# Reading the moving operand of one-pass products from two halves in turn

## The chip, the cores and the metric

The kernel runs on one core of one Trainium2 chip. The metric is the device time of one execution in microseconds (us). Engines are named as the profile names them: PE is the matrix engine (TensorE), PEld its weight loads, DVE the vector engine, ACT the scalar engine, POOL the GpSimd engine, SP the engine that issues most transfers. L977 is line 977 of the kernel before.

## The reference

Two stages follow each other. First a long convolution with a filter that a small network makes, gated by x:

```python
h_filt = (np.maximum(pos_emb @ w1, 0.0) @ w2) * np.exp(-0.01 * pos)[:, None]
u = x * v                                   # x, v: [2, 12480, 128]
y = irfft(rfft(u, 2 * S) * rfft(h_filt, 2 * S))[:, :S]
z = x * y                                   # [24960, 128] after a reshape
```

Then an MLP with a leaky ReLU on every row of z:

```python
h = z @ w_in                                # [24960, 128] @ [128, 2048]
g = np.maximum(0.01 * h, h)
out = g @ w_out                             # [24960, 2048] @ [2048, 128]
```

Everything is float32.

## The kernel before

The convolution is done as a transform over 98 x 128 points in two steps, a product with the filter's spectrum, and the way back. Batch 0's convolution and the filter's spectrum fill the time up to about 337 us. From there on the MLP runs, and the rest of the convolution (batch 1 and the last inverse transforms) is woven between the MLP's steps.

The MLP works on 50 column tiles of tokens: 46 of 512 columns and four ends of 390, 314, 352 and 352 (`widths`). For each tile it makes 16 steps, one for every 128 of the 2,048 hidden units. A step has two parts. `m1` multiplies the tile by 128 columns of `w_in`, and the result is passed through the ReLU on ACT and split into a high part `rh` and a low part `rl`. `m2`, issued three steps later (`DEEP`), multiplies `rh` and `rl` by `w_out` and adds into the tile's accumulator `acc`. Every operand is held as a high and a low float32r part, so each logical product is three products on PE: high by high, high by low, low by high. [...] The other products (`conv1`, `fwd`, `back_halves`, `last_transform`, the transposes) use plain float32 operands; the rows below show what one of their columns takes.

For 21 of the 50 tiles (`sums(k)`) the leaky ReLU is split as 0.99 relu(h) + 0.01 h, with the second term folded into three products by `wc_h` and `wc_l` (L1006 to L1008). There ACT writes `rh` straight from PSUM (L981) and DVE makes `rl` from PSUM and `rh` (L982). For the other 29 tiles ACT makes `r` from PSUM (L990), and ACT or DVE casts it to `rh` (L994, L992); DVE makes `rl` from the two (L995) without reading PSUM.

The result of a tile stands in `acc`. `finish` copies it on ACT in pieces (L1025) into tiles `ot` of 390 tokens, which PE transposes back to rows (L1037) and SP stores.

Batch 1's second convolution stage (`conv1b`) has two places with one-pass products, both through `three` (L138): the forward product `up`, read by ACT and DVE at L522, L524 and L528, and the way back, `back`, whose result ACT copies at L210 in `back_evac`.

The order is written out by hand: a program order for each engine, with `pace` handing out the pieces of batch 1's convolution among the MLP's steps, and tables (`ends`, `turn_at`, `gets`) that place the last transforms.

Of the kernel before, what the change touches and what calls it, by code (L numbers as in the profile page):

```python
# [12 lines left out]
AF = mybir.ActivationFunctionType  # L13
# [17 lines left out]
def tile_conv_mlp(ctx, tc, x, v, pos_emb, w1, w2, w_in, w_out, cf, cr, cg, cb, ci, cw, out):  # L31
# [81 lines left out]
            pass  # L113


    def chunk(c):
        k0 = c * KC
        return k0, min(KC, NA - k0)
# [27 lines left out]
    def back_halves(dp, pin, c):  # L146

        for j, w in halves(c):
            for s in range(2):
                rows = slice(HB * s, HB * s + HB)  # L150
                for ri in range(2):
                    nc.tensor.matmul(dp[s][:, w], mi2[j][rows, ri, :], pin[rows, ri, w],
                                     start=(ri == 0), stop=(ri == 1))

    def back(dp, parts, c):

        for s in range(2):
            for j, w in halves(c):
                three(dp[s][:, w], (mi_h[j][:, s], mi_l[j][:, s]), (parts[0][:, s, w], parts[1][:, s, w]))

    def turned(pool, psum, m2, m1):

# [39 lines left out]
    def store_back(b, c, ct, eng):  # L202
        k0, n = chunk(c)
        eng.dma_start(out=scr2[b][k0:k0 + n].rearrange("k r m e -> (r m) k e"),
                          in_=ct[:, :n].rearrange("p k s d -> p k (s d)"))

    def back_evac(dp, ct, n):

# [5 lines left out]
    with tc.manual_schedule():  # L214
# [237 lines left out]
        def conv1b():  # L452

            pool = psc["pool"]
            hd, parts = {}, {}

            def fetch_b(c):
                if c < NCH:
                    k0, n = chunk(c)
                    got[c] = s0.tile([128, 1024], F32, tag="s1", name="bin1", bufs=3).rearrange(  # L460
                        "p (k s d) -> p k s d", s=2, d=D)
                    nc.sync.dma_start(out=got[c][:, :n].rearrange("p k s d -> p k (s d)"),
                                      in_=scr1b[:, k0:k0 + n, :])

            def fetch_h(c):
                n = chunk(c)[1]
                h = pool.tile([128, 2, 2, 512], F32, tag="hd", name="hd")
                for i in range(2):
                    nc.sync.dma_start(out=h[HB * i:HB * i + HB, :, :, :n * D], in_=hspec[c][:, :, :, :n * D])
                hd[c] = h  # L470

            def split(c):
                _, n = chunk(c)
                t = got.pop(c)
                th = pool.tile([128, KC, 2, D], F32R, tag="th", name="th", bufs=1)
                tl = pool.tile([128, KC, 2, D], F32R, tag="tl", name="tl", bufs=1)
                parts[c] = th, tl
                nc.scalar.copy(th[:, :n, 0, :], t[:, :n, 0, :])
                yield
                for s in range(2):  # L480
                    if s == 0:
                        nc.scalar.copy(th[:, :n, 1, :], t[:, :n, 1, :])
                    nc.vector.tensor_tensor(out=tl[:, :n, s, :], in0=t[:, :n, s, :], in1=th[:, :n, s, :],
                                            op=ALU.subtract)
                    yield

            def sums(us, p1, h, s, w):
                nc.gpsimd.tensor_tensor(out=us[:, s, :w], in0=us[:, s, :w], in1=h[:, 1, s, :w], op=ALU.mult)
                nc.gpsimd.tensor_tensor(out=p1[:, s, :w], in0=p1[:, s, :w], in1=us[:, s, :w], op=ALU.add)

            fetch_b(0)
            fetch_h(0)
            fetch_b(1)
            fetch_b(2)
            for _ in range(WAIT):
                yield
            yield from split(0)
            late, pins = None, {}
            for c in range(NCH + 1):
                if c + 1 < NCH:  # L500
                    fetch_h(c + 1)
                if late:
                    late()
                    late = None
                if c < NCH:
                    n = chunk(c)[1]
                    w = n * D
                    h, (th, tl) = hd.pop(c), parts.pop(c)
                    yield
                    up = psc["next"]()  # L510
                    for s in range(2):
                        three(up[s][:, :w].rearrange("p (k d) -> p k d", d=D), (mb_h[:, s], mb_l[:, s]),
                              (th[:, :n, s, :], tl[:, :n, s, :]))
                    yield

                    us, p1 = sc.tile([128, 2048], F32, tag="s4", name="usp").rearrange(
                        "a (i s w) -> i a s w", i=2, s=2)
                    ph = pool.tile([128, 2, 512], F32R, tag="ph", name="ph", bufs=1)
                    pl = pool.tile([128, 2, 512], F32R, tag="pl", name="pl", bufs=1)
                    pins[c] = ph, pl  # L520
                    for s in range(2):
                        nc.scalar.mul(us[L, s, :w], up[s][H, :w], -1.0)  # L522
                        o = 1 - s
                        nc.vector.tensor_tensor(out=p1[:, o, :w], in0=up[o][:, :w], in1=h[:, 0, o, :w], op=ALU.mult)  # L524
                        if s:
                            sums(us, p1, h, 0, w)
                        yield
                        nc.scalar.copy(us[H, s, :w], up[s][L, :w])  # L528
                        yield
                    sums(us, p1, h, 1, w)  # L530
                if c + 1 < NCH:
                    yield from split(c + 1)
                    fetch_b(c + 3)
                if c:
                    wb = chunk(c - 1)[1] * D
                    dp = psc["next"]()
                    back(dp, pins.pop(c - 1), c - 1)
                    yield
                    ct = pool.tile([128, KC, 2, D], F32, tag="ct1", name="ct1", bufs=1)
                    yield from back_evac(dp, ct, wb // D)  # L540
                    late = lambda c=c, ct=ct: store_back(1, c - 1, ct, nc.sync)
                    yield
                if c < NCH:
                    for s in range(2):
                        nc.scalar.copy(ph[:, s, :w], p1[:, s, :w])
                        nc.gpsimd.tensor_tensor(out=pl[:, s, :w], in0=p1[:, s, :w], in1=ph[:, s, :w],
                                                op=ALU.subtract)
                        yield
            late()
# [419 lines left out]

        def m1(k, f):  # L970
            w = widths[k]
            zh, zl = (i[:, :w] for i in z[k])
            hp = ps.tile([128, WIDE], F32, tag="mh", name="mh", bufs=3)[:, :w]
            fs = slice(f * 128, f * 128 + 128)
            for i, (u, m) in enumerate(((w_in_h, zh), (w_in_l, zh), (w_in_h, zl)) if k == f == 0 else
# [2 lines left out]
            rh = sm.tile([128, WIDE], F32R, tag="rh", name="rh", bufs=DEEP + 2)[:, :w]  # L978
            rl = sm.tile([128, WIDE], F32R, tag="rl", name="rl", bufs=DEEP + 2)[:, :w]
            if sums(k):  # L980
                nc.scalar.activation(out=rh, in_=hp, func=AF.Relu)  # L981
                nc.vector.scalar_tensor_tensor(out=rl, in0=hp, scalar=0.0, in1=rh, op0=ALU.max, op1=ALU.subtract)  # L982
            else:
                tag, pool, bufs = ((("th", psc["pool"], 1), ("tl", psc["pool"], 1), ("ct1", psc["pool"], 1),
                                    ("ph", psc["pool"], 1), ("pl", psc["pool"], 1)) if k in OWN else
                                   (("s1", s0, 3), ("hd", psc["pool"], 2), ("ct1", psc["pool"], 1),
                                    ("s1", s0, 3), ("hd", psc["pool"], 2)))[f % 5]
                r = pool.tile([128, 2048 if tag == "hd" else 1024], F32R if tag in ("th", "tl", "ph", "pl") else F32,
                              tag=tag, name="r", bufs=bufs)[:, :w].bitcast(F32)
                nc.scalar.activation(out=r, in_=hp, func=AF.Lrelu, alpha=0.01)  # L990
                if f % 2:
                    nc.vector.tensor_copy(rh, r)  # L992
                else:
                    nc.scalar.copy(rh, r)  # L994
                nc.vector.tensor_tensor(out=rl, in0=r, in1=rh, op=ALU.subtract)  # L995
            return rh, rl

        def m2(k, f, r):
            rh, rl = r
            w = widths[k]  # L1000
            if f == 0:
                acc[k] = ps.tile([128, WIDE], F32, tag=f"acc{k % 2}", name="acc", bufs=1)
            if f == 0 and sums(k):
                zh, zl = (i[:, :w] for i in z[k])
                ap = acc[k][:, :w]
                nc.tensor.matmul(ap, wc_h, zh, start=True, stop=False)  # L1006
                nc.tensor.matmul(ap, wc_h, zl, start=False, stop=False)
                nc.tensor.matmul(ap, wc_l, zh, start=False, stop=False)  # L1008
# [7 lines left out]
        def finish(k):  # L1016
# [3 lines left out]
            for t in range(at0[k] // TOK, (at0[k + 1] - 1) // TOK + 1):  # L1020
                for kk, a, c, n in pieces_of(t):
                    if kk == k:
                        if t not in ots:
                            ots[t] = sm.tile([128, TOK], F32, tag="ot", name="ot", bufs=3)
                        nc.scalar.copy(ots[t][:, c:c + n], ap[:, a:a + n])  # L1025
                        if c + n == TOK:
                            whole.append(t)
            for t in whole:
# [243 lines left out]
```

## Time and profile before

| | |
|---|---|
| median of three executions | 1689.55 us (1683.47 to 1690.23) |
| the profiled execution's own time | 1684.68 us |
| its span, first to last instruction | 1682.9 us |
| mean granted TensorE clock | 0.988 |
| busy: PE, PEld, DVE, ACT, POOL | 97%, 78%, 71%, 60%, 49% |

The span is what the trace covers; 1.8 us of the execution lie outside of it. A row of the trace gives an instruction's line, engine, operation, output and inputs by the program's names, and its shape: `128*128 128x512` is a product with 128 x 128 weights and 512 moving columns. The end of a matrix product is modelled, and one product starts before the one ahead of it has ended, so a product's own duration (0.39 us) is not what it costs: the distance from one start to the next is.

### The profile page before, as it was taken

How to read it: one execution, taken by the hardware profiler on the slowest of the kernel's cores; microseconds unless marked ns; L12 is line 12 of the kernel's file. 1: busy time of each engine (PE TensorE's matmuls, PEld its weight loads, DVE VectorE, ACT ScalarE, POOL GpSimd, SP SyncE). 2: the span in 40 equal slices, each digit the busy share in tenths (PEclk: the TensorE clock that was granted, in tenths of full speed). 3: DMA queues.
4: the chain of work that ended last, by engine and by line, in shares of the span. 5: the costliest groups of instructions: out<-in, count | busy, mean ns of one | idle time of the engine just before them, and what ended most of it. 6: DMA issues, size and time to landing. Idle time of an engine off the chain costs nothing.

```text
span 1682.9 us, 27337 instructions
## 1 busy us (share of the span) xinstructions
PE 1628.1 (97%) x9173; PEld 1319.2 (78%) x9173; DVE 1193.9 (71%) x1785; ACT 1008.0 (60%) x2056; POOL 821.6 (49%) x804
## 2 busy tenths in 40 slices
PE   6897999899999999999999999999999999999999
PEld 6786555488888888888888888888888888887888
DVE  4775888656775566666566664887887887878765
ACT  1332454345654577676677676666667676676666
POOL 3563212245643376767567763654464545445410
PEclk9998999999999999999999999999999999999999
DMA  8898999766766466656566631321212212121100
GB/s 237 285 301 248 342 321 342 253 195 186 209 177 196 124 170 196 192 157 171 155 177 165 167 105 55 122 68 56 61 61 66 75 53 75 56 61 56 56 11 20
DMA packets 166357, 253.30 MB, mean 151 GB/s; under 512 B 14302, under 2 KB 119026, under 8 KB 163146
## 3 DMA queue, kind: packets, MB, share of 16 engines
q1 hardware_dynamic: 146478, 226.29, 45.6%
q10 hardware_dynamic: 19740, 25.28, 4.3%
q8 instruction: 73, 1.20, 0.3%
q14 instruction: 66, 0.54, 0.1%
HBM read 168.00 MB, written 83.43 MB: 149 GB/s over the span
## 4 chain that ended last, share of the span: by engine, by line
PE 79%; DVE 9%; DMA 7%; issue 2%; ACT 1%; SPq 1%; POOL 0%; ACTq 0%; DVEq 0%; POOLq 0%
PE mh L977 30%; PE acc L1011 10%; PE acc L1012 10%; PE acc L1010 10%; PE cv L138 4%; PE yp L903 4%; PE cv L425 3%; DMA scr<-o 2%; DMA ft<-in_cf_dram 2%; PE op L1037 2%; PE zp L922 1%; PE up L124 1%; DVE rl L995 1%; DVE ta L132 1%; PE a L381 1%
## 5 line engine op out<-in xcount | busy, mean ns | idle before, releaser
L995 DVE TENSOR_TENSOR rl<-r,rh 128x512 fp32r<-128x512 f32 (+2 forms) x464 | 398.1, 875 | 101.0 <-ACT rh L994 92.4
L990 ACT ACTIVATE r<-mh 128x512 f32<-128x512 f32 (+2 forms) x464 | 271.3, 586 | 193.8 <-PE mh L977 175.2
L982 DVE SCALAR_TENSOR_TENSOR rl<-mh,rh 128x512 fp32r<-128x512 f32 (+1 forms) x336 | 227.8, 683 | 222.9 <-ACT rh L981 220.6
L977 PE MATMUL mh<-zh,w_in_h 128*128 128x512 f32 (+3 forms) x800 | 327.6, 410 | 0.8 <-ACT zh L966 0.7
L1011 PE MATMUL acc<-rl,w_out_h 128*128 128x512 f32 (+3 forms) x800 | 309.6, 387 | 1.3 <-DVE rl L995 0.6
L977 PE MATMUL mh<-zh,w_in_l 128*128 128x512 f32 (+3 forms) x800 | 310.3, 388 | 0.0
L1010 PE MATMUL acc<-rh,w_out_h 128*128 128x512 f32 (+3 forms) x800 | 310.3, 388 | 0.0
L1012 PE MATMUL acc<-rh,w_out_l 128*128 128x512 f32 (+3 forms) x800 | 309.9, 387 | 0.0
L977 PE MATMUL mh<-zl,w_in_h 128*128 128x512 f32 (+3 forms) x800 | 309.4, 387 | 0.0
L981 ACT ACTIVATE rh<-mh 128x512 fp32r<-128x512 f32 (+1 forms) x336 | 199.7, 596 | 157.3 <-PE mh L977 151.4
L936 POOL TENSOR_TENSOR zl<-zf,zh 128x390 fp32r<-128x390 f32 (+24 forms) x110 | 69.3, 643 | 406.1 <-ACT zh L935 401.0
L666 POOL TENSOR_TENSOR cp<-cq,cp 98x256 f32<-98x256 f32 x248 | 223.0, 899 | 34.4 <-DVE cp L654 17.7
L992 DVE CAST rh<-r 128x512 fp32r<-128x512 f32 (+2 forms) x232 | 146.5, 632 | 48.6 <-ACT r L990 47.3
L1011 PEld LDWEIGHTS acc<-rl,w_out_h 128*128 128x128 f32 x800 | 150.3, 188 | 38.5 <-DVE rl L995 7.0
L977 PEld LDWEIGHTS mh<-zh,w_in_l 128*128 128x128 f32 x800 | 150.7, 188 | 32.1
L977 PEld LDWEIGHTS mh<-zh,w_in_h 128*128 128x128 f32 x800 | 151.2, 189 | 31.1 <-issue 3.9
L1012 PEld LDWEIGHTS acc<-rh,w_out_l 128*128 128x128 f32 x800 | 150.3, 188 | 30.7
L1010 PEld LDWEIGHTS acc<-rh,w_out_h 128*128 128x128 f32 x800 | 150.4, 188 | 30.2
L977 PEld LDWEIGHTS mh<-zl,w_in_h 128*128 128x128 f32 x800 | 151.5, 189 | 24.1 <-DVE zl L968 0.2
L994 ACT CAST rh<-r 128x512 fp32r<-128x512 f32 (+2 forms) x232 | 140.9, 607 | 7.3
L663 POOL TENSOR_TENSOR cq<-cin 98x256 f32<-98x256 f32 x124 | 120.1, 968 | 0.8 <-DMA cin<-scr 0.8
L654 POOL TENSOR_TENSOR cp<-cin 98x256 f32<-98x256 f32 x78 | 74.6, 975 | 66.3 <-PE yp L903 32.0
(165 smaller groups left out, 2390.1 us busy)
## 6 DMA issues: line engine op xcount, KB each, us to landing
cin<-scr SPq DMA_DIRECT2D x318, 98.0 KB
hd<-hspec SPq DMA_DIRECT2D x48, 512.0 KB
bin<-scr SPq DMA_DIRECT2D x23, 768.0 KB
scr<-o SPq DMA_DIRECT2D x28, 588.0 KB
scr<-ct SPq DMA_DIRECT2D x25, 512.0 KB
scr1b<-o SPq DMA_DIRECT2D x32, 392.0 KB
hspec<-hs ACTq DMA_DIRECT2D x48, 256.0 KB
xm<-in_x_dram SPq DMA_DIRECT2D x128, 96.0 KB
```

The costliest lines, as they stand in the source:

```text
L663: eng.tensor_tensor(out=cq[:, p], in0=ci_t[:, 0, :, 0, :], in1=ci_t[:, 0, :, 1, :], op=op)
L666: eng.tensor_tensor(out=cp[:, p, w], in0=cq[:, p], in1=cp[:, p, 1], op=op)
L977: nc.tensor.matmul(hp, u[:, fs], m, start=(i == 0), stop=(i == 2))
L981: nc.scalar.activation(out=rh, in_=hp, func=AF.Relu)
L982: nc.vector.scalar_tensor_tensor(out=rl, in0=hp, scalar=0.0, in1=rh, op0=ALU.max, op1=ALU.subtract)
L990: nc.scalar.activation(out=r, in_=hp, func=AF.Lrelu, alpha=0.01)
L992: nc.vector.tensor_copy(rh, r)
L994: nc.scalar.copy(rh, r)
L995: nc.vector.tensor_tensor(out=rl, in0=r, in1=rh, op=ALU.subtract)
L1010: nc.tensor.matmul(ap, w_out_h[:, f, :], rh, start=(f == 0 and not sums(k)), stop=False)
L1011: nc.tensor.matmul(ap, w_out_h[:, f, :], rl, start=False, stop=False)
L1012: nc.tensor.matmul(ap, w_out_l[:, f, :], rh, start=False, stop=(f == NF - 1))
```

## The change

Three helpers are added. `mixed` reads a tile of 2n columns in the order 0, n, 1, n+1, ...; `plain` takes a result that stands in that order in PSUM and gives it back as two halves, each read with a step of two; `split2` is the same pair of halves on a tile in plain order.

```diff
+    def mixed(t):
+        return t.rearrange("p (h i) -> p i h", h=2)
+    def plain(t):
+        return t.rearrange("p (i h) -> p h i", h=2)
+    def split2(t):
+        return t.rearrange("p (h i) -> p h i", h=2)
+    def even(w):
+        return (w.stop - w.start) // D % 2 == 0
```

In the MLP the moving operands of all products are read through `mixed`, and all that read their results do it through `plain`:

```diff
         def m1(k, f):
-            zh, zl = (i[:, :w] for i in z[k])
+            zh, zl = (mixed(i[:, :w]) for i in z[k])
...
-                nc.scalar.activation(out=rh, in_=hp, func=AF.Relu)
-                nc.vector.scalar_tensor_tensor(out=rl, in0=hp, scalar=0.0, in1=rh, op0=ALU.max, op1=ALU.subtract)
+                nc.scalar.activation(out=split2(rh), in_=plain(hp), func=AF.Relu)
+                nc.vector.scalar_tensor_tensor(out=split2(rl), in0=plain(hp), scalar=0.0, in1=split2(rh),
+                                               op0=ALU.max, op1=ALU.subtract)
...
-                nc.scalar.activation(out=r, in_=hp, func=AF.Lrelu, alpha=0.01)
+                nc.scalar.activation(out=split2(r), in_=plain(hp), func=AF.Lrelu, alpha=0.01)
...
         def m2(k, f, r):
-            rh, rl = r
+            rh, rl = (mixed(i) for i in r)
...
-                zh, zl = (i[:, :w] for i in z[k])
+                zh, zl = (mixed(i[:, :w]) for i in z[k])
...
-                        nc.scalar.copy(ots[t][:, c:c + n], ap[:, a:a + n])
+                        half = widths[k] // 2
+                        for h in range(2):
+                            lo, hi = max(a, half * h), min(a + n, half * h + half)
+                            if lo < hi:
+                                nc.scalar.copy(ots[t][:, c + lo - a:c + hi - a],
+                                               plain(ap[:, :2 * half])[:, h, lo - half * h:hi - half * h])
```

In `conv1b` the same is done for the forward products and, where a group holds an even number of 128-column blocks, for the products of the way back:

```diff
-                        three(up[s][:, :w].rearrange("p (k d) -> p k d", d=D), (mb_h[:, s], mb_l[:, s]),
-                              (th[:, :n, s, :], tl[:, :n, s, :]))
+                        three(up[s][:, :w], (mb_h[:, s], mb_l[:, s]),
+                              [i[:, :n, s, :].rearrange("p (h k) d -> p k d h", h=2) for i in (th, tl)])
...
-                        nc.scalar.mul(us[L, s, :w], up[s][H, :w], -1.0)
+                        nc.scalar.mul(split2(us[L, s, :w]), plain(up[s][H, :w]), -1.0)
-                        nc.vector.tensor_tensor(out=p1[:, o, :w], in0=up[o][:, :w], in1=h[:, 0, o, :w], op=ALU.mult)
+                        nc.vector.tensor_tensor(out=split2(p1[:, o, :w]), in0=plain(up[o][:, :w]),
+                                                in1=split2(h[:, 0, o, :w]), op=ALU.mult)
-                        nc.scalar.copy(us[H, s, :w], up[s][L, :w])
+                        nc.scalar.copy(split2(us[H, s, :w]), plain(up[s][L, :w]))
...
     def back(dp, parts, c):
-                three(dp[s][:, w], (mi_h[j][:, s], mi_l[j][:, s]), (parts[0][:, s, w], parts[1][:, s, w]))
+                m = mixed if even(w) else lambda t: t
+                three(dp[s][:, w], (mi_h[j][:, s], mi_l[j][:, s]), (m(parts[0][:, s, w]), m(parts[1][:, s, w])))
```

`mixed_evac` takes the place of `back_evac` there: the same copies, with a step of two where the group is even; the one chunk that is cut into odd groups gets two copies for each half instead of one.

## Rows read from the trace of the kernel before

**Rows 1.** The page, part 1: busy time and share of the span.
```profile
PE 1628.1 (97%) x9173; PEld 1319.2 (78%) x9173; DVE 1193.9 (71%) x1785; ACT 1008.0 (60%) x2056; POOL 821.6 (49%) x804
```

**Rows 2.** Windows: stretch, length, busy time and instructions, granted clock, DMA share, GB/s.
```profile
core 0: us, PE busy (x) PEld busy (x) DVE busy (x) ACT busy (x) POOL busy (x), PEclk, DMA share, GB/s
184.00:188.00 4.00, 3.73 (x40) 2.34 (x37) 2.51 (x5) 2.41 (x6) 1.29 (x1) 1.00 0.99 366
600.00:700.00 100.00, 100.00 (x502) 81.54 (x501) 63.32 (x92) 70.59 (x145) 71.41 (x71) 1.00 0.69 190
1200.00:1300.00 100.00, 99.90 (x504) 81.33 (x503) 80.19 (x103) 70.02 (x141) 47.05 (x51) 1.00 0.19 56
```

**Rows 3.** Groups by line and form, whole span: count, busy us, mean ns, idle before.
```profile
L977 PE MATMUL mh<-zh,w_in_h 128*128 128x512 f32 x736 | 304.9, 414 | 0.1
L1006 PE MATMUL acc<-zh,wc_h 128*128 128x512 f32 x20 | 7.8, 392 | 0.0
L977 PE MATMUL mh<-zh,w_in_h 128*128 128x352 f32 x32 | 10.6, 330 | 0.0
L138 PE MATMUL cv<-th,mb_h 128*128 128x512 f32 x48 | 19.3, 402 | 0.0
L138 PE MATMUL cv<-ph,mi_h 128*128 128x512 f32 x46 | 18.6, 403 | 0.0
```

**Rows 4.** Timeline, PE, two MLP steps (start us, duration us): first and last product.
```profile
1199.80 0.39 PE L977 MATMUL mh<-zh,w_in_h 128*128 128x512 f32 x1
...
1202.32 0.39 PE L1012 MATMUL acc<-rh,w_out_l 128*128 128x512 f32 x1
```

**Rows 5.** Timeline, PE: from the first `up` product to what follows the sixth.
```profile
588.20 0.40 PE L138 MATMUL cv<-th,mb_h 128*128 128x512 f32 x1
...
589.59 0.39 PE L977 MATMUL mh<-zh,w_in_h 128*128 128x512 f32 x1
```

**Rows 6.** Timeline, PE, 352 columns: the first and the ninth of a run.
```profile
1664.02 0.32 PE L1010 MATMUL acc<-rh,w_out_h 128*128 128x352 f32 x1
...
1665.30 0.32 PE L1012 MATMUL acc<-rh,w_out_l 128*128 128x352 f32 x1
```

**Rows 7.** Timeline, PE: float32 products merged, and what starts after them.
```profile
184.98 1.94 PE L124 MATMUL up<-bin,mb 128*64 128x512 f32 x8 [0.27 <-DVE ta L132]
186.72 1.07 PE L769 MATMUL ep<-mb,bin 128*64 128x128 f32 x16
...
383.37 1.91 PE L425 MATMUL cv<-xv,ft 98*98 98x128 f32 x16
385.04 0.47 PE L977 MATMUL mh<-zh,w_in_h 128*128 128x512 f32 x1
```

**Rows 8.** Groups by form: readers of PSUM (first four), then DVE in the weights' preparation.
```profile
L990 ACT ACTIVATE r<-mh 128x512 f32<-128x512 f32 x325 | 195.3, 601 | 147.1 <-PE mh L977 132.9 <-DVE rl L995 2.3
L990 ACT ACTIVATE r<-mh 128x352 f32<-128x352 f32 x32 | 15.0, 468 | 7.7 <-PE mh L977 7.7
L982 DVE SCALAR_TENSOR_TENSOR rl<-mh,rh 128x512 fp32r<-128x512 f32 x161 | 109.9, 689 | 100.3 <-ACT rh L981 99.7
L982 DVE SCALAR_TENSOR_TENSOR rl<-mh,rh 128x390 fp32r<-128x390 f32 x16 | 8.9, 563 | 7.4 <-ACT rh L981 7.2
L91 DVE SCALAR_TENSOR_TENSOR fs<-wo,fa 128x256 uint32<-128x256 uint32 x8 | 3.4, 426 | 0.3
L98 DVE TENSOR_TENSOR wo<-fa,fb 128x256 f32<-128x256 f32 x8 | 3.4, 425 | 0.3
```

**Rows 9.** Groups by form: ACT in 600 to 900 us, then DVE in 1100 to 1600 us.
```profile
L522 ACT ACTIVATE usp<-cv 64x512 f32<-64x512 f32 x34 | 20.3, 597 | 2.6 <-PE cv L138 1.6
...
L995 DVE TENSOR_TENSOR rl<-r,rh 128x512 fp32r<-128x512 f32 x324 | 290.0, 917 | 58.0 <-ACT rh L994 51.8
L992 DVE CAST rh<-r 128x512 fp32r<-128x512 f32 x163 | 109.3, 671 | 36.6 <-ACT r L990 35.9
```

**Rows 10.** Waits in total (us, times, longest), and the last copy in the timeline.
```profile
PEld acc L1011 <- DVE rl L995: 7.0, 15, 0.7
...
1678.25 0.45 ACT L1025 COPY ot<-acc 128x352 f32<-128x352 f32 x1 [1.61 <-PE acc L1012]
```

More of the change, by code (lines that the diff above doesn't have):

```diff
@@ L205, in store_back, with mixed_evac @@
                           in_=ct[:, :n].rearrange("p k s d -> p k (s d)"))
+    def mixed_evac(dp, ct, c):
+        for s in range(2):
+            for _, w in halves(c):
+                o, i = ct[:, w.start // D:w.stop // D, s, :], dp[s][:, w]
+                if even(w):
+                    nc.scalar.copy(o.rearrange("p (h k) d -> p h k d", h=2),
+                                   i.rearrange("p (k d h) -> p h k d", h=2, d=D))
+                else:
+                    nc.scalar.copy(o, i.rearrange("p (k d) -> p k d", d=D))
+            yield
     def back_evac(dp, ct, n):
@@ L539, in conv1b @@
                     ct = pool.tile([128, KC, 2, D], F32, tag="ct1", name="ct1", bufs=1)
-                    yield from back_evac(dp, ct, wb // D)
+                    yield from mixed_evac(dp, ct, c - 1)
                     late = lambda c=c, ct=ct: store_back(1, c - 1, ct, nc.sync)
```

## The prediction

> **What bounds the kernel now.** I read the busy times first, then the windows, then the starts of PE's products in the timeline, and last the groups of those that read PE's results. PE is busy for 97% of the span, the next engine, DVE, for 71% [rows 1]. [...]
>
> What a product costs is the distance between starts. Twelve of the MLP's products of 512 columns start within 1199.80 to 1202.32 us, eleven distances: 2.52 / 11 = 0.2291 us each [rows 4]. [...]
>
> [...]
>
> **The change part by part.**
>
> *The order in which products read.* Each product reads as many columns as before, now n, n+256, n+1, ... [...] The count: six lines of 736 products of 512 columns and three of 20 [rows 3] make 4,476, each 13.1 ns shorter: 58.6 us. The conv products, three of 48 and three of 46 [rows 3], 282 in all, from 231.7 to 216: 4.4 us. The 192 of 352 columns (six of 32 [rows 3]) from 160 to 148.5, the same price for a column: 2.2 us. The tiles of 390 and 314, 96 products and a few each, at some 10 ns (an estimate by their width): 2 us. Together 67 us. [...]
>
> [...]
>
> *The readers of PSUM with a step of two.* ACT reads each MLP result once (L981 or L990), DVE those of 21 tiles too (L982), and ACT and DVE the convolution's. ACT pays (601 - 468) / 160 = 0.83 ns a column and DVE (689 - 563) / 122 = 1.03 [rows 8]. Below, the step costs nothing: DVE reads 256 words with a step of two at L91 in 426 ns and 256 neighbours at L98 in 425 [rows 8], though from SBUF. Above, every column takes twice its price: 427 and 529 ns more for 512. I take nothing, by the nearest rows. What they write, and the second operands in SBUF, are two runs of 256 neighbours. Cover: ACT is busy for 70% and DVE for 63 to 80% of the MLP's time [rows 2]; the price without cover is the third rival.
>
> *More copies.* `finish` makes 111 copies now; cut where a piece crosses the middle of its tile they are 161, and one chunk of `mixed_evac` has 2 more. Each costs ACT its start, 601 - 512 x 0.83 = 176 ns: 9 us over 1,340, hidden in ACT's 30% idle. Only the last lies on the path to the end: 0.45 us of copy at 1678.25 [rows 10] becomes two, at most 0.2 us more.
>
> *What the shorter step runs into.* No transfer, weight load or step is moved or added; the queues keep their order. But a step of six products falls from 1.375 to 1.296 us, and DVE has 0.917 for each `rl` and half of 0.671 for the casts it shares with ACT in the later 26 tiles, 1.25 us by means of rows [rows 9]. These means hold some overlap (busy 290.0 / 324 = 0.895, so 1.23). Between two transforms, DVE then has 0.06 us a step left where it had 0.14. With `m2` three steps behind this holds, but waits of PE for `rl`, 7.0 us in the present run [rows 10], may grow; I give back 3 us.
>
> Sum against the profiled execution: 1684.7 - 67 + 0.2 + 3 = 1621. That execution lies 5 us below the median of the three; I keep to it, and a median after may stand as far above.
>
> **The rivals.**
>
> [...]
>
> [...]
>
> *Step two costs the readers double.* In 600 to 900 us ACT is busy for 70% [rows 2]; 161 MLP results (L982's count [rows 8]) and 34 x 3 conv reads (L522 and the like [rows 9]) at 427 ns more are 112 us in 300: 107% of the present time. Later, 325 in 500 us [rows 8] make 70 + 28 = 98%. ACT becomes the bound: about +30 us over the convolution's stretch (600 to 1033), the gain elsewhere nearly gone, near 1710 us. Against it: L91.
>
> **How the numbers follow.** Half a per cent, 8 us, is about what a measurement of this kernel can tell from no change. My forecast, faster to 1621, has 0.65, with its own range from 1603 (all 81 us) to 1655 (under half of the excess goes). Two cycles a column: 0.17. The order does not matter: 0.12. Readers at double price: 0.06. So faster 0.65, same 0.12, slower 0.23. The range for eight in ten takes the forecast and the two near rivals, 1600 to 1712; it leaves out the two-cycle case, whose price lies far off.
>
> **What would show it.** The distance between starts of `mh` and `acc` products: 0.216 for 0.229 if I am right, 0.229 if the order is nothing, 0.43 if each turn costs a cycle. The float32 products' distances should not move. L990 and L981 near 601 ns and L982 near 689 show that the step of two is free. ACT's L1025 count should be 161. If products come at 0.216 and the time falls by much less than 60 us, the place to look is PE waiting for `rl` (L995) in the later tiles. The prediction is wrong if the distance does not fall below 0.225.

## The result and the profile after

The changed kernel takes 1630.9 us (median of four, 1629.69 to 1635.63) against 1687.64 us for the kernel before on the same chip (median of four): a ratio of 0.968, 95% interval 0.966 to 0.970. The forecast was 1621, the range 1600 to 1712. The profiled execution of after took 1631.98 us, its span 1630.2, 52.7 us less than before.

PE's rows in the timeline of after (start us, duration us, engine, line, operation): first and twelfth product of two MLP steps, first and sixth forward product of the convolution, first and ninth of a run of 352 columns, then the float32 products. L1007 is L977 of before; L1041 to L1043 are L1010 to L1012, L150 is L138, L136 is L124, L454 is L425. Of the other engines, L1021 is L990, L1011 and L1012 are L981 and L982, L1026 is L995 and L1060 is L1025.

```profile
1199.36 0.38 PE L1007 MATMUL mh<-zh,w_in_h 128*128 128x512 f32 x1
...
1201.74 0.38 PE L1043 MATMUL acc<-rh,w_out_l 128*128 128x512 f32 x1
...
609.26 0.38 PE L150 MATMUL cv<-th,mb_h 128*128 128x512 f32 x1
...
610.34 0.38 PE L150 MATMUL cv<-th,mb_l 128*128 128x512 f32 x1
...
1610.71 0.31 PE L1043 MATMUL acc<-rh,w_out_l 128*128 128x352 f32 x1
...
1611.90 0.31 PE L1007 MATMUL mh<-zl,w_in_h 128*128 128x352 f32 x1
...
184.94 1.94 PE L136 MATMUL up<-bin,mb 128*64 128x512 f32 x8 [0.22 <-DVE ta L144]
186.68 1.07 PE L799 MATMUL ep<-mb,bin 128*64 128x128 f32 x16
...
380.35 1.91 PE L454 MATMUL cv<-xv,ft 98*98 98x128 f32 x16
382.02 0.46 PE L1007 MATMUL mh<-zh,w_in_h 128*128 128x512 f32 x1
```

One-pass products is the name here for those of the float32r parts; what the rows show of them is the distance between their starts. Eleven distances in 2.38 us are 0.2164 us each, where before had 0.2291 [rows 4]; the 13 ns between the two, 14.0 by the means over both traces, are the excess that the experiments look for. The convolution's are 1.08 / 5 = 0.216, where they had 0.2317 [rows 5]; at 352 columns 1.19 / 8 = 0.149, where before had 0.160 [rows 6]. The float32 products stand as they did: 1.74 us for eight of 512 columns and 1.67 for sixteen of 128, in both kernels [rows 7].

The readers of PSUM, groups by line and form (count, busy us, mean ns, idle before), and the copies of `finish` by line:

```profile
L1021 ACT ACTIVATE r<-mh 128x512 f32<-128x512 f32 x416 | 249.0, 599 | 152.3 <-PE mh L1007 132.9 <-DVE rl L1026 9.2 <-DVE zt L943 3.5
L1012 DVE SCALAR_TENSOR_TENSOR rl<-mh,rh 128x512 fp32r<-128x512 f32 x320 | 217.8, 688 | 191.7 <-ACT rh L1011 190.8
L1060 ACT COPY ot<-acc x161: 172/301/405, 363.1 to 1625.9; 128x256 f32<-128x256 f32 x32, 128x38 f32<-128x38 f32 x3, 128x176 f32<-128x176 f32 x3, 128x195 f32<-128x195 f32 x2
```

With a step of two ACT takes 599 ns and DVE 688, as they did with neighbours, 601 and 689 [rows 8]. (The counts differ because [rows 8] has L990 in 1100 to 1600 us and L982 in 600 to 900 us only; over the whole span their means are the same.) There are 161 copies.

What is new stands in the windows (stretch, length, busy time and instructions, clock, DMA) and in the waits (us in total, times, longest):

```profile
600.00:700.00 100.00, 97.63 (x511) 83.52 (x510) 64.67 (x91) 69.87 (x147) 76.49 (x73) 1.00 0.71 198
1200.00:1300.00 100.00, 98.81 (x539) 83.25 (x538) 84.18 (x106) 71.06 (x144) 53.83 (x57) 1.00 0.22 68
```

```profile
PEld acc L1042 <- DVE rl L1026: 23.3, 50, 0.9
PEld mh L1007 <- DVE rl L1012: 8.6, 17, 1.2
PE acc L1042 <- DVE rl L1026: 6.2, 21, 0.5
PE mh L1007 <- DVE rl L1012: 2.4, 5, 0.8
```

PE, which had no gap in 600 to 700 us, now has 2.4 us there and 1.2 in 1200 to 1300 [rows 2], and the weight load for the product with `rl` waits for DVE for 23.3 us, where it waited for 7.0 [rows 10]. The loads for the products into `mh` wait for L1012 for 8.6 us, 2.6 in the kernel before (there L982). A wait of the load costs time only where PE itself starts late for it, which the two PE lines show in part: they count idle time only from a product's modelled end. One such wait in the timeline:

```profile
1546.08 2.25 DVE L1026 TENSOR_TENSOR rl<-r,rh 128x512 fp32r<-128x512 f32 x2
...
1546.56 0.38 PE L1041 MATMUL acc<-rh,w_out_h 128*128 128x512 f32 x1
1546.60 2.34 POOL L684 TENSOR_TENSOR cp<-cin 98x256 f32<-98x256 f32 x2
...
1547.24 0.48 PE L1042 MATMUL acc<-rl,w_out_h 128*128 128x512 f32 x1 [0.30 <-DVE rl L1026]
```

DVE makes two `rl` in 2.25 us while POOL sums, and PE's products at 1546.56 and 1547.24 are 0.68 apart instead of 0.216.

### The profile page after: what moved, and what is told of

It is laid out like the page before. It is cut to its first block, busy times and chain, and to the rows that moved or that the text cites. A ratio compares the mean times of both kernels' runs of the same rounds, so it can differ in the third digit from the quotient of the medians.

```text
span 1630.2 us, 27296 instructions
## 1 busy us (share of the span) xinstructions
PE 1566.8 (96%) x9173; PEld 1318.9 (81%) x9173; DVE 1185.8 (73%) x1785; ACT 1010.4 (62%) x2108; POOL 818.0 (50%) x804
## 4 chain that ended last, share of the span: by engine, by line
PE 62%; DVE 13%; DMA 11%; ACT 5%; issue 5%; SPq 2%; POOL 2%; ACTq 0%; DVEq 0%; POOLq 0%
PE mh L1007 23%; PE acc L1042 8%; PE acc L1043 7%; PE acc L1041 7%; DVE rl L1026 4%; PE yp L933 4%; PE cv L150 3%; DVE rh L1023 3%; PE cv L454 3%; DMA scr<-ct 2%; DMA vt<-in_v_dram 2%; DMA pos<-in_pos_emb_dram 2%; PE op L1073 1%; PE zp L952 1%; PE up L136 1%
## 5 line engine op out<-in xcount | busy, mean ns | idle before, releaser
L1026 DVE TENSOR_TENSOR rl<-r,rh 128x512 fp32r<-128x512 f32 (+2 forms) x464 | 396.7, 873 | 83.6 <-ACT rh L1025 56.7
L1021 ACT ACTIVATE r<-mh 128x512 f32<-128x512 f32 (+2 forms) x464 | 270.6, 585 | 162.7 <-PE mh L1007 139.4
L1012 DVE SCALAR_TENSOR_TENSOR rl<-mh,rh 128x512 fp32r<-128x512 f32 (+1 forms) x336 | 226.7, 682 | 198.7 <-ACT rh L1011 197.7
L1007 PE MATMUL mh<-zh,w_in_h 128*128 128x512 f32 (+3 forms) x800 | 316.8, 396 | 3.5 <-DVE rl L1012 2.4
L1042 PE MATMUL acc<-rl,w_out_h 128*128 128x512 f32 (+3 forms) x800 | 304.2, 380 | 6.6 <-DVE rl L1026 6.2
L1007 PE MATMUL mh<-zl,w_in_h 128*128 128x512 f32 (+3 forms) x800 | 300.0, 375 | 0.2 <-POOL zl L966 0.2
L1007 PE MATMUL mh<-zh,w_in_l 128*128 128x512 f32 (+3 forms) x800 | 299.8, 375 | 0.0
L1041 PE MATMUL acc<-rh,w_out_h 128*128 128x512 f32 (+3 forms) x800 | 299.2, 374 | 0.0
L1043 PE MATMUL acc<-rh,w_out_l 128*128 128x512 f32 (+3 forms) x800 | 299.1, 374 | 0.0
L1011 ACT ACTIVATE rh<-mh 128x512 fp32r<-128x512 f32 (+1 forms) x336 | 198.8, 595 | 133.3 <-PE mh L1007 124.6
L1042 PEld LDWEIGHTS acc<-rl,w_out_h 128*128 128x128 f32 x800 | 151.2, 189 | 42.1 <-DVE rl L1026 23.3
L1007 PEld LDWEIGHTS mh<-zh,w_in_h 128*128 128x128 f32 x800 | 151.8, 190 | 29.6 <-DVE rl L1012 8.6
L1007 PEld LDWEIGHTS mh<-zh,w_in_l 128*128 128x128 f32 x800 | 151.8, 190 | 19.6
L1041 PEld LDWEIGHTS acc<-rh,w_out_h 128*128 128x128 f32 x800 | 151.3, 189 | 19.8
L1043 PEld LDWEIGHTS acc<-rh,w_out_l 128*128 128x128 f32 x800 | 151.4, 189 | 18.4
L1007 PEld LDWEIGHTS mh<-zl,w_in_h 128*128 128x128 f32 x800 | 152.2, 190 | 15.7 <-POOL zl L966 0.6
L1025 ACT CAST rh<-r 128x512 fp32r<-128x512 f32 (+2 forms) x232 | 140.2, 604 | 7.4
```

Source lines behind the costliest of these rows:

```text
L1007: nc.tensor.matmul(hp, u[:, fs], m, start=(i == 0), stop=(i == 2))
L1011: nc.scalar.activation(out=split2(rh), in_=plain(hp), func=AF.Relu)
L1012: nc.vector.scalar_tensor_tensor(out=split2(rl), in0=plain(hp), scalar=0.0, in1=split2(rh), op0=ALU.max, op1=ALU.subtract)
L1021: nc.scalar.activation(out=split2(r), in_=plain(hp), func=AF.Lrelu, alpha=0.01)
L1041: nc.tensor.matmul(ap, w_out_h[:, f, :], rh, start=(f == 0 and not sums(k)), stop=False)
L1042: nc.tensor.matmul(ap, w_out_h[:, f, :], rl, start=False, stop=False)
```

## The experiments

In runs 1 to 6 and 9 the results of the MLP leave PSUM in another order of tokens; they are read for their time alone. Runs 3 to 7 and 9 were executed once each. The rows are PE's timeline in each: the first and the last of a run of products, with the number of distances told behind. In runs 3 to 6 and 9, L1009 and L1043 to L1045 are L1007 and L1041 to L1043 of the changed kernel. The cuts show the lines for the MLP; the reads and copies of the convolution that go with them are left out.

**1 and 2. Which half of the change acts?** One run takes the new order of reading and lets ACT and DVE read PSUM as before; the other does the reverse.

```diff
 # run 1, from the changed kernel
     def plain(t):
-        return t.rearrange("p (i h) -> p h i", h=2)
+        return t.rearrange("p (h i) -> p h i", h=2)
 # run 2, from the changed kernel
     def mixed(t):
-        return t.rearrange("p (h i) -> p i h", h=2)
+        return t
```

> The products read two halves in turn as in the changed kernel, and all that read PSUM read neighbours, as in the kernel before (so tokens come out in another order; only the time is read). Theory A, the excess of a one-pass product comes from the order in which its moving columns are read: products of 512 columns start 0.216 us apart, and the time is that of the changed kernel, 1631 +- 5 us. Theory B, the excess comes from ACT and DVE reading PSUM in neighbour order while PE writes it: 0.229 apart and 1685 +- 5 us. If the step of two costs the readers something, L1011, L1012 and L1021 get shorter than 600, 688 and 599 ns, and the time falls below 1626.

> The products read neighbours as in the kernel before, and all that read PSUM take a step of two, as in the changed kernel (so tokens come out in another order; only the time is read). Theory A: products start 0.229 us apart, 1686 +- 5 us. Theory B: 0.216 apart, 1631 +- 5 us.

Run 1 took 1635.7 us, a ratio to the kernel before of 0.969 (0.966 to 0.972); run 2 took 1684.3, a ratio of 0.9996 (0.998 to 1.001). Run 1, then run 2:

```profile
500.57 0.38 PE L1007 MATMUL mh<-zl,w_in_h 128*128 128x512 f32 x1
...
502.73 0.38 PE L1043 MATMUL acc<-rh,w_out_l 128*128 128x512 f32 x1
```

```profile
503.64 0.40 PE L1007 MATMUL mh<-zl,w_in_h 128*128 128x512 f32 x1
...
505.94 0.40 PE L1043 MATMUL acc<-rh,w_out_l 128*128 128x512 f32 x1
```

Ten distances each: 0.216 and 0.230. The order in which the moving columns are read brings the whole gain; theory B falls. The step of two neither helps nor costs: in both runs ACT and DVE take 599 to 601 and 688 to 689 ns for what reads PSUM.

**3 and 4. What about the order?** The two places are put 16 bytes apart, or there is one place with steps of 16 bytes.

```diff
     def mixed(t):
-        return t.rearrange("p (h i) -> p i h", h=2)
+        return t.rearrange("p (b h i) -> p b i h", h=2, i=4)     # run 3: 0 4 1 5 2 6 3 7, 8 12 ...
+        return t.rearrange("p (i h) -> p h i", h=4)              # run 4: 0 4 8 ... 508, 1 5 ...
```

> MLP products of 512 and 352 columns read in blocks of eight, 0 4 1 5 2 6 3 7, so turns are 16 bytes apart instead of 1 KB; products of 390 and 314 columns and the convolution's read neighbours; readers of PSUM take neighbours (tokens in another order; only the time is read). Theory A in its simple form, that two neighbours one right after the other stall: 0.216 us between starts, about 1636 us. Theory A2, that the two places must be far from each other (other banks of the memory): 0.229, about 1685. [...]

> MLP products of 512 and 352 columns read with a step of four columns, 0 4 8 ... 508 1 5 ..., so that each read is 16 bytes on and no two reads in a row are neighbours, but there are no turns between two places; the rest as in the run with blocks of eight. Theory A in its simple form: 0.216 us between starts, about 1636 us. If the turn between two places is what helps: 0.229 or more. [...]

One point in these expectations is not exact: of the convolution's products, those of the way back read in the new order too, here and in runs 5, 6 and 9. The MLP's decide. Run 3 took 1637.3 us, run 4 2770.0:

```profile
499.67 0.38 PE L1044 MATMUL acc<-rl,w_out_h 128*128 128x512 f32 x1
...
501.18 0.38 PE L1045 MATMUL acc<-rh,w_out_l 128*128 128x512 f32 x1
```

```profile
499.73 0.66 PE L1009 MATMUL mh<-zh,w_in_h 128*128 128x512 f32 x1
...
504.79 0.66 PE L1045 MATMUL acc<-rh,w_out_l 128*128 128x512 f32 x1
```

Seven distances of 0.216 and eleven of 0.460. So 16 bytes are far enough for the turn to help (0.216), and theory A2 falls. The simple form of theory A falls too: run 4 has no two neighbours in a row, and its products take 0.460, twice the time. What it does not have is a second read of the same 16 bytes soon after the first. Going to other 16 bytes with each read is not in itself what costs: run 3 does so too, at 0.216. Below, a line is only a name for 16 bytes in a row, four columns, the step of these two runs.

**5, 6 and 9. Within 16 bytes, and with more places.**

```diff
+        return t.rearrange("p (b h i) -> p b i h", h=2, i=2)     # run 5: 0 2 1 3, 4 6 5 7, ...
+        return t.rearrange("p (h i) -> p i h", h=8)              # run 6: eight places in turn
+        return t.rearrange("p (h i) -> p i h", h=4)              # run 9: four places in turn
```

> MLP products of 512 and 352 columns and the way-back products read in blocks of four, 0 2 1 3, so every turn stays within 16 bytes; readers of PSUM take neighbours (tokens in another order; only the time is read). If it is enough that no two reads in a row are neighbours: 0.216 us between starts, about 1637 us. If the turn must be to another 16-byte line, as the run with 16-byte turns and the one with a step of four leave open: 0.229, about 1685.

> MLP products of 512 and 352 columns read eight places in turn, n/8 columns apart, instead of two; each line of 16 bytes is come back to after eight reads (tokens in another order; only the time is read). If a line once read stays at hand however many others come between: 0.216 us, about 1637 us. If only a few lines stay at hand: towards the 0.460 us that a step of four took, up to 2770 us.

> MLP products of 512 and 352 columns and the way-back products read four places in turn, n/4 columns apart (tokens in another order; only the time is read). If the lines of two places are all that stays at hand: near the 0.460 to 0.487 us that a step of four and eight places took, about 2770 to 2900 us. If four stay at hand: 0.216 us, about 1637 us. A distance between the two would mean a price of each turn that grows with the places.

One point in the first of them is not exact: run 5 has neighbours in a row, 2 1 and 3 4, at half of its steps. They took 1684.6, 2900.5 and 1895.9 us. In this order:

```profile
500.77 0.39 PE L1009 MATMUL mh<-zl,w_in_h 128*128 128x512 f32 x1
...
503.06 0.39 PE L1045 MATMUL acc<-rh,w_out_l 128*128 128x512 f32 x1
```

```profile
499.75 0.69 PE L1043 MATMUL acc<-rh,w_out_h 128*128 128x512 f32 x1
...
503.64 0.69 PE L1045 MATMUL acc<-rh,w_out_l 128*128 128x512 f32 x1
```

```profile
500.67 0.44 PE L1009 MATMUL mh<-zl,w_in_h 128*128 128x512 f32 x1
...
505.10 0.45 PE L1045 MATMUL acc<-rh,w_out_l 128*128 128x512 f32 x1
```

Ten distances of 0.229, eight of 0.486, sixteen of 0.277. A turn that stays within 16 bytes does nothing (0.229), though half of the pairs of neighbours are gone. With four places in turn each line is come back to after four reads and the product costs more than with neighbours, 0.277 for 0.229; with eight it costs somewhat more even than with run 4's steps of 16 bytes, 0.486 for 0.460. Two places in turn, at 0.216, are the fastest of the orders tried. One thing these runs leave untested: with the number of places their distance changes too, 512 bytes for four and 256 for eight. For two places the distance made no difference (1 KB and 16 bytes, both 0.216); for four and eight it was not varied.

**7. The rival at the weight load.** Each product loads weights while the one ahead of it runs: in the kernel before a load starts at 1200.04 us and takes 0.19, beside the product that starts at 1200.03, and its own product starts at 1200.26. In run 7, that kernel with the edit, one load of six has half its columns.

```diff
+                if i == 1:
+                    nc.tensor.matmul(hp[:64], u[:, f * 128:f * 128 + 64], m, start=False, stop=False)
+                    continue
                 nc.tensor.matmul(hp, u[:, fs], m, start=(i == 0), stop=(i == 2))
```

> The kernel before, but the second of the three products of m1 (zl by w_in_h) loads and uses 64 weight columns instead of 128 (half of the hidden units lose their low part; only the time is read). Theory A, the excess comes from the order of the moving columns alone: L977's products zh by w_in_h, beside which the half load runs, and zl by w_in_h both stay at 0.229 to 0.231 us. Theory C, the excess comes from the weight load that reads beside the moving columns: the product beside the half load starts its follower after about 0.222, the others stay.

It took 1687.7 us. Its timeline, the first four and the last of the twelve products of two steps:

```profile
1203.31 0.39 PE L980 MATMUL mh<-zh,w_in_h 128*128 128x512 f32 x1
1203.54 0.39 PE L978 MATMUL mh<-zl,w_in_h 128*64 128x512 f32 x1
1203.77 0.40 PE L980 MATMUL mh<-zh,w_in_l 128*128 128x512 f32 x1
...
1205.84 0.39 PE L1015 MATMUL acc<-rh,w_out_l 128*128 128x512 f32 x1
```

A full load and the one with half its columns, as groups (count, busy us, mean ns, idle before):

```profile
L980 PEld LDWEIGHTS mh<-zh,w_in_l 128*128 128x128 f32 x799 | 150.4, 188 | 71.5
...
L978 PEld LDWEIGHTS mh<-zl,w_in_h 128*64 128x64 f32 x799 | 108.3, 136 | 23.3
```

The product beside the half load is 0.23 from its follower, as all are (2.53 / 11). Over all its products the mean is 228.5 ns, 2.6 less than before, while the other five moved by -1.4 to +2.1; the six together moved by some 2 ns, where theory C had 9 from the one. That speaks against theory C as the main cause, but the test is weaker than planned: the load with half its columns took 136 ns, not half of 188, and a price that every load has whatever its length would not show here. What is shown is run 1: with every load in place, the new order alone takes the excess away. Whether the old order and the loads get in each other's way is not shown.

**8 and 10. Where the rest of the gain went.** Half as many casts on DVE, in the changed kernel and in the one before.

```diff
-                if f % 2:
+                if f % 4 == 1:
                     nc.vector.tensor_copy(rh, r)
```

> The changed kernel with every fourth cast of r on DVE (f % 4 == 1) instead of every second one; the rest of them on ACT. Theory: in the later tiles DVE has 1.23 us of work for a step that now takes 1.296, and PE waits for rl for about 20 us; with 0.16 us a step less on DVE these waits go, ACT rises from 71% to about 81% busy, and the time falls from 1631 to about 1618 us. Rival: the waits come from the slow rl beside POOL's sums alone, or ACT, which now casts in a row with the ReLU, becomes late instead: 1628 to 1640.

> The kernel before, with every fourth cast of r on DVE instead of every second one. Theory: there DVE has 1.23 us of work for a step of 1.375, PE waits for rl for 5 us only, so the time falls by 3 to 6 us, 1680 to 1683, and the gain of 13 us that the same edit gave in the changed kernel belongs to the shorter step. Rival: DVE's share was a cost of its own in both: 1670 to 1675.

The changed kernel with this edit takes 1618.1 us (1616.24 to 1621.11), a ratio to before of 0.960 (0.958 to 0.963), clear of the changed kernel's 0.966 to 0.970. The kernel before with it takes 1680.3, a ratio of 0.997 (0.996 to 0.998). A window and the waits for `rl` in the first of them:

```profile
1200.00:1300.00 100.00, 100.00 (x576) 87.03 (x573) 80.36 (x92) 81.69 (x167) 56.71 (x59) 1.00 0.23 71
```

```profile
PEld mh L1007 <- DVE rl L1012: 8.5, 17, 1.1
PE mh L1007 <- DVE rl L1012: 2.3, 5, 0.7
PEld acc L1042 <- DVE rl L1026: 1.7, 5, 0.6
PE acc L1042 <- DVE rl L1026: 0.2, 1, 0.2
```

The waits for L1026, of both engines added, go from 29.5 us to 1.9, PE is busy without a gap again in this window, and ACT stands at 82% where 81 was expected. In the kernel before the same edit brings 5 to 6 us, as its expectation had it (3 to 6), against 13 in the changed one. So by the times some 7 of the 13 us are the price of the shorter step (some 10 by the MLP's stretch in the profiled executions, which got 14.9 and 4.4 us shorter), and the rest was there already: the rival of run 10 falls, but "the gain of 13 us belongs to the shorter step" was too much. The waits for L1012, in the stretch where the convolution is woven in, stay; what makes L1012 late there was not tried.

## Why the prediction was right, and what it mis-sized

*What bounds the kernel.* Right: in the MLP's windows PE was busy for 99.9 to 100 us of 100 [rows 2], with its products closer together the time fell, and no transfer took their place (DMA share 0.71 and 0.22 in the two windows of after, 0.69 and 0.19 before).

*The order of reading.* Right in place and close in size, wrong in the reason. No row shows the 0.216 on which the 13.1 ns and the step of 1.296 us rest, nor the 81 us at the lower end of the forecast's own range. The traces show 215.8 ns as the mean of products of 512 columns back to back, near enough to 0.216 by luck. Against the mean of 229.8 before, this is 14.0 ns, not 13.1: 62.7 us on the 4,476 products, where I had 58.6. With the convolution's 282 (233.8 by the mean, 5 us) and the narrow ones (4 us) the products gave 72 us, where I had 67, and no run gave the 81. The reason that I had for it, theory A in its simple form, is half right. The excess goes with the order in which the moving columns are read, and 14.0 ns a product are gone where they come from two lines in turn. That neighbours stall, and that more time between them frees the products, is not what the runs show: run 4 has no neighbours in a row and takes 0.460, run 5 has half as many and the same 0.229, and run 9, with four reads from one neighbour to the next, takes 0.277.

*Readers with a step of two.* Right: nothing (599 for 601 ns and 688 for 689), as L91 had it.

*More copies.* Right: 161, hidden. The last two take 0.51 us where the one took 0.45 [rows 10].

*What the shorter step runs into.* This is the term that was mis-sized: I gave back 3 us, and the trace gives back some 18. Adding up, over all products of 512 columns that follow another one-pass product, what a distance has over the usual one by more than 25 ns gives 5.2 us before, 22.8 after and 7.7 in run 8. I had seen DVE's 0.06 us of slack for a step, and took it by means. But DVE's `rl` is not 0.9 us each time: it has two levels. L995 of before and L1026 of the changed kernel from 1100 to 1600 us (ns: least, median, most; the least of the second belongs to the few of 352 columns) show the lower one in the median and the upper in the most:

```profile
L995 DVE TENSOR_TENSOR rl<-r,rh x324: 677/694/1239, 1100.2 to 1598.5; 128x512 fp32r<-128x512 f32 x162
```

```profile
L1026 DVE TENSOR_TENSOR rl<-r,rh x340: 524/693/1230, 1099.3 to 1599.1; 128x512 fp32r<-128x512 f32 x168, 128x352 fp32r<-128x352 f32 x2
```

The other is the 2.25 us for two beside POOL's sums, shown with the result, 1.13 each. Over the whole trace of the changed kernel, the `rl` of 512 columns beside which POOL is busy for under 0.3 of their time, 223 of 416, take 0.69 us on average. Those of the upper level come mostly in rows of four to eleven steps. There DVE needs 1.13 and half a cast of 0.67 [rows 9], an estimate of 1.47 us for a step. That is more than 1.296, and more than the 1.375 of before too: by this estimate DVE lost its lead of three steps in the kernel before as well, by 0.09 us a step instead of 0.17, and such a row of steps mostly ended before PE had to wait. In the changed kernel the product with `rl` comes over 40 ns late 31 times, in the one before 11 times, and each time at least two of the last three `rl` were of the upper level.

Not all of the 18 us are of this kind. Some 11 were added at the product with `rl` and the one behind it (4.3 us before, 15.7 after, 0.6 in run 8). Some 5 were added at the product behind the last one of a step, where PE mostly waits for L1012 (0.3, 5.3 and 5.3); run 8 leaves them, and their cause stays open. Stage by stage: the MLP's stretch, from the first `mh` to the last `acc` product, shrank from 1340.6 to 1289.6 us, 51 us: 72 of gain, 18 of waits, and 3 that I can't place.

*The rivals.* The order does not matter, and readers at double price: neither holds, by run 1's 0.216 and by the readers' 599 and 688 ns. Two cycles a column, the 0.43 of the prediction's last part, is wrong for this order, which takes 0.216; that it would be cycles, no run shows. But orders with a price of that size exist: runs 4 and 6 take 0.460 and 0.486, and 2770 and 2900.5 us in all.

*What stays open.* Why neighbours cost 14 ns more at 512 columns than turns between two lines, no run shows; it goes with the order of the moving columns and not with who reads PSUM, and a part of the weight load in it is neither shown nor excluded. Nor does it follow the columns plainly: the new order took off 14 ns at 512 columns, 10.8 at 352 and 11.7 at 314. Run 4's steps take 244 ns more than the new order at 512 columns; whether these two prices have one cause is not shown.

## What to carry to other kernels

Look at the distance between the starts of products, not at their durations (0.216 and 0.38 us here). The order in which an operand is read is worth an experiment, and it is free to choose when the readers of the result can undo it at no cost. Two places in turn, 16 bytes or 1 KB apart, made one-pass products some 6% shorter here (0.216 for 0.229); four places or a step of 16 bytes made them 21% and 100% longer (0.277 and 0.460). When the bound engine gets faster, take the slack of the next one from its slowest stretch, and from how long that stretch lasts, not from its mean.

## What the runs showed of the hardware

One-pass products of 512 columns, at a mean granted clock of 0.984 to 0.992 over each execution: 0.229 us apart with neighbours or with turns within 16 bytes, 0.216 with two places in turn (1 KB or 16 bytes apart), 0.277 with four, 0.486 with eight, 0.460 with steps of 16 bytes. That a turn between two lines is the fastest of the orders tried, and that the price with four places lies between, I had not expected. ACT and DVE read PSUM with a step of two at the price of neighbours, 599 for 601 and 688 for 689 ns. A DVE subtraction with both inputs in SBUF took 0.69 us for 512 columns, and 1.1 to 1.2 beside POOL's sums.
